# One FFN chunk normalized in transposed layout, a pair's inverse stage cut by columns, and a table turned by DMA

## The chip, the cores and the metric

The kernel runs on one core of a Trainium2 chip. The metric is the device time of one execution in microseconds. A core has five engines, each with its own queue of instructions: TensorE (PE, matrix products out of SBUF into PSUM; its weight loads are shown as PEld), VectorE (DVE), ScalarE (ACT), GpSimd (POOL), and SyncE (SP), which here issues all DMA transfers. An instruction waits at the head of its queue until the semaphores it needs are up; those behind it wait with it.

## What is computed

```python
x = A_x                                        # 1 x 2048 x 512, bf16
X = rfft2(layernorm(x)) * (A_w_r + 1j * A_w_i)
h = x + irfft2(X, (2048, 512)).astype(bf16)
u = layernorm(h)
r = relu(u @ B_w1 + B_b1)                      # 512 -> 1792
out = h + (r * r) @ B_w2 + B_b2                # 1792 -> 512
```

A layernorm takes off the mean over the 512 features and divides by sqrt(variance + 1e-5).

## The kernel before

Token 16 p + g lies on partition p, in group g (16 groups of 128 tokens). The two-dimensional transform is done as matrix products with tables of sines and cosines that the kernel makes itself.

- *Front.* x arrives in six transfers. For each group DVE (bn_stats) or ACT takes mean and variance; POOL raises the variance to the power -1/2; the first table KF is scaled by it (KR, L409). Stage 1 (s1, L416 and L417) multiplies each group by KR, and the result goes into Bt (L432, L448). The row means stay in nm1 with their sign turned; what the filter adds has a row mean of zero, so nm1 serves the second layernorm too.
- *Middle.* Eight pairs of frequency blocks, pr = 0 to 7. For each: stage 2 on PE with table GF (p2, L516), its eviction U on ACT (L526), stage 3 with table EF (p3, L495), its eviction AB on ACT (L593), then on DVE a butterfly X (L600, for the pairs that do it there), the product m with the filter weights W (L614), the complex combination Z in two halves (L624), and a fold M in two halves (L635, L637; pair 6 has none and takes Z itself). Stage 4 (p4) multiplies by the inverse table EI (L662; pair 6 in L659 also by EN, a negated slice), and T2 is its eviction (L677). p4 of pair 7 is made in two parts, each of half of the row table index; each part's eviction is cut into the columns of groups 0 and 1 (T2a) and of the others (T2b).
- *Drain, for the tokens of chunk 0 (groups 0 and 1).* Stage 5 with table GI (pd, L738) needs T2a of all pairs. Its evictions EO (L743) go into stage 6 with table KI (py, L828 to L833), which is accumulated on top of x. Group 0 gets its sum of squares on ACT (L689), group 1 its statistics by bn_stats on DVE (L843); then square root on ACT (L846), reciprocal, scaled offset, the normalized u (L857, L859), a transpose on PE through the identity (L868), and a copy to UT (L874). Then come the up products.
- *FFN.* Five chunks of groups, (0, 2), (2, 5), (5, 9), (9, 13), (13, 16). Up products ph/sg (L936), relu on ACT (L948), square on DVE (L954), down products po (L965), addition of hb on DVE (L974), output by SP. Stages 5 and 6 of the later groups (p5, L765 to L768; p6, L788 to L796) and their second layernorm are woven between.

The tables: EF and GF are sines by ACT from integer phases. EI0 and EI1 are EF turned by DMA (`tr_dma`, L453), EI2 is EI0 negated on ACT (L482), EN a negated slice on ACT (L485). GI is made directly: POOL makes its phases fiI (L469), ACT takes the sine (L260, at 35.5 in the profile).

*What sets the order.* All work is given to a planner, `Plan`, as tasks with an engine, an assumed duration, what it reads and writes, a priority and a pool slot. `plan.run` chooses at each step the task that can start first by its own assumed times, and emits it; the emitted order is then fixed for each engine (`pin`). In the middle the order is instead written out by hand for PE, ACT and DVE (`MID`). An assumed duration is not a time of the chip; it only decides the order. Transfers have assumed landing times (`lag`). When the planner sees a gap in front of a product it puts in products of zeros (`warm`, L243, and the loop in `bank`, L716), whose result is overwritten.

PSUM has eight banks: in the middle three double banks (mm) and two single ones (sg); in the FFN three pp, one ph, two po, two sg.

Of the kernel before, what the change touches and what calls it, by code (L numbers as in the profile page):

```python
# [9 lines left out]
ALU = mybir.AluOpType  # L10
# [23 lines left out]
class Plan:  # L34
# [55 lines left out]
    def run(self, line=None):  # L90
# [8 lines left out]
        while any(left.values()):  # L99
            best = None  # L100
            for e, ts in left.items():
                cand = []
                for t in ts if e not in lines else [t for t in ts if t["name"] == lines[e][0]] if lines[e] else []:
                    r = self.ready(t, e)
                    if r is None:
                        continue
                    if t["alloc"]:
                        s, _ = self.slot(t["alloc"][0])
                        if s is None:
                            continue  # L110
                        r = max(r, s)
                    r = max(r, self.free[e])
                    cand.append((r, t))
                    if r <= self.free[e] + 1e-9:
                        break
# [17 lines left out]
            if e in lines:  # L133
                lines[e].pop(0)
# [10 lines left out]
def kernel(  # L145
# [22 lines left out]
    BY_Z = (6,)  # L168
    L = D // 2
# [23 lines left out]
    mv2 = persist.tile([P, 2], FP32, name="mv2")  # L193
    st2 = persist.tile([P, 6], FP32, name="st2")
# [10 lines left out]
    EI = fwd.tile([P, 3, 9, P], BF16, name="EI")  # L205
    EN = fwd.tile([P, len(BY_Z), 2, P], BF16, name="EN")
# [20 lines left out]
    fiI = tab.tile([P, 4, 256], I32, name="fiI")  # L227
    idxD = tab.tile([P, 256], I32, name="idxD")
# [57 lines left out]
    for i in range(2):  # L286
        add("SP", 1.0, lambda i=i: sy.dma_start(W[:, 2 + i, 1:8], wx[i][:, ::-1]), reads=[("wx", i)], writes=[("Wr", i)],
            prio=10 + i, lag=10.5)
# [27 lines left out]
    pool(0.14, lambda: iota(pI[:, 5:7], [[128, 2]], 128, 256), 1.0, writes=["p2"])  # L316
# [4 lines left out]
    pool(0.34, lambda: iota(idxD[:], [[1, 256]], 0, 0), 395.0, writes=["idxD"], order=[("KR", G - 1)])  # L321
# [31 lines left out]
    for t in range(2):  # L353
        act(0.62, lambda t=t: sin_of(flat(GF[:, t]), lo(flat(fiG[:, t]))), 0.6 + t / 10, reads=[("fiG", t)],
            writes=[("gf", t)])
    dve(0.15, lambda: ve.tensor_scalar(GF[:, :, :, 255:256], GF[:, :, :, 255:256], 0.5, None, ALU.mult), 54.0, reads=[("gf", 0), ("gf", 1)],
        order=[("KR", G - 1)], writes=["GF"])
# [94 lines left out]
    def tr_dma(i, dst, src, dep, prio):  # L452
        add("SP", 2.5, lambda: sy.dma_start(dst, src, transpose=True), reads=dep, writes=[("EI", i)], prio=prio, lag=(10.6, 10.4, 0, 8.0)[i])  # L453
    for i in range(2):
        tr_dma(i, EI[:, i], flat(EF[:, i]), [f"EF{i}"], 12 + i)
    tr_dma(3, KI[:], flat(KF[:]), ["KF"], 16)
    for k, (d, s) in ((0, (W1[:], B_w1.rearrange("(c p) f -> p c f", p=P))),
# [3 lines left out]
            order=[("EI", i) for i in range(4)] + [("Wr", 0), ("Wr", 1), ("Wn", 0), ("Wn", 1)])  # L461
# [5 lines left out]
    dve(0.13, lambda: ve.tensor_copy(pF[:, 5:7], pI[:, 5:7]), 0.75, reads=["p2"], writes=["pF2"], shared=True)  # L467
    for lt in range(4):
        pool(0.48, lambda lt=lt: gp.tensor_scalar(fiI[:, lt], idxD[:], pF[:, 5 + lt % 2:6 + lt % 2],  # L469
                                                  float((QT, HT)[lt // 2]), ALU.mult, ALU.add), 400.0,  # L470
             reads=["pF2", "idxD", ("KR", G - 1)], writes=["fiI"])
# [5 lines left out]
    def mid_tasks():  # L477
        def b1t():
            mm(sg_tile(("b1",))[:, 0:NF], lhsT=b1b[:], rhs=ident[0:NF, 0:NF], start=True, stop=True)
        add("PE", 0.07, b1t, reads=["b1b", "ident"], order=[("p3", 3)], writes=[("b1",)], prio=141.0, alloc=("sg", ("b1",)))  # L480
        act(0.19, lambda: sc.copy(b1f[:], T[("b1",)][:, 0:NF]), 142.0, reads=[("b1",)], writes=["b1f"])
        act(1.1, lambda: sc.activation(flat(EI[:, 2]), flat(EI[:, 0]), ACT.Identity, scale=-1.0), 83.0, reads=[("EI", 0)],  # L482
            order=["EF2", ("X", 0, 0)], writes=[("EI", 2)])
        for pr in BY_Z:
            act(0.37, lambda pr=pr: sc.activation(EN[:, BY_Z.index(pr)], EI[:, 0:2, pr], ACT.Identity, scale=-1.0), 84.0,  # L485
                reads=[("EI", 0), ("EI", 1)], writes=[("EI", 3, pr)])
        act(1.07, lambda: sin_of(flat(GI[:]), lo(flat(fiI[:]))), 142.0, reads=["fiI"], order=[("p3", 4)], writes=["GI"])
        act(1.4, lambda: sc.activation(junk[:, 0:1], eps[:], ACT.Sqrt), 0.0, reads=["GI", "eps", ("p4", SQ)], writes=["sqrt"])
# [8 lines left out]
    for pr, first in ((0, 1), (1, 1), *((p, 0) for p in range(8))):  # L497
# [12 lines left out]
        if first or pr > 1:  # L510
# [7 lines left out]
            for q in range(2):  # L518
                add("PE", 0.46, lambda pr=pr, q=q, s2=s2: s2(pr, q), reads=["Bt", "GF"],
# [102 lines left out]
        def zz(pr=pr, r=0):  # L622
            Z = buf(fwd, ("Z", pr), "Z", [P, 2, 2, 256], BF16, 2) if r == 0 else T["Z", pr]
            ve.tensor_tensor(Z[:, :, r], T["m", pr][:, :, 0, r], T["m", pr][:, :, 1, 1 - r], (ALU.subtract, ALU.add)[r])  # L624
# [18 lines left out]
        def s4(pr, part, lts):  # L643
            key = ("p4", pr, "t", lts[0] // 2) if pr == 7 else ("p4", pr)
            pt = T[key] if part else (sg_tile if pr == 7 else mm_tile)(key)
            src = T["M" if pr and pr not in BY_Z else "Z", pr][:].rearrange("p u r (j e) -> p u r e j", e=2)
            for lt in lts:
                r, e = lt // 2, lt % 2
                k = lt - lts[0] if pr == 7 else lt
                o = pt[:, 256 * k:256 * k + 256]  # L650
                if pr == 0:
                    for u, k1 in ((0, 0), (1, 8)):
                        ou = o[:, P * u:P * u + P]
                        mm(ou, lhsT=src[:, u, r, e, :], rhs=EI[:, 1, k1, :], start=True, stop=False)
                        mm(ou, lhsT=src[:, u, 1 - r, e, :], rhs=EI[:, 2 if r == 0 else 0, k1, :], start=False, stop=True)
                elif pr in BY_Z:
                    for u in range(2):
                        i = 1 if r == part else 0 if u != r else 2
                        mm(o, lhsT=src[:, u, part, e, :], rhs=EI[:, i:i + 2, pr, :] if i < 2 else EN[:, BY_Z.index(pr)],  # L659
                           start=part == 0 and e == 0 and u == 0, stop=part == 1 and e == 1 and u == 1)  # L660
                else:
                    mm(o, lhsT=src[:, part, r, e, :], rhs=EI[:, 1 - part:3 - part, pr, :],  # L662
                       start=part == 0 and e == 0, stop=part == 1 and e == 1)
        for h in range(2):
            for k in range(2) if pr == 7 else (None,):
                lts = {None: range(4) if pr else (2 * h, 2 * h + 1), 0: (0, 1), 1: (2, 3)}[k]
                add("PE", 0.92 if pr in BY_Z else 0.46 if k is None else 0.23, lambda pr=pr, h=h, s4=s4, lts=lts: s4(pr, h, lts),
                    reads=[("Z", pr) if pr == 0 else ("ZM"[pr not in BY_Z] + "h" * (1 - h), pr), ("EI", 0), ("EI", 1), ("EI", 2)]
                    + [("EI", 3, pr)] * (pr in BY_Z), order=[("p4", pr, 0, k)] * h, uses=[("ZM"[pr > 0 and pr not in BY_Z], pr)],
                    writes=[("p4", pr, h, k)] + [("p4", pr)] * (k is None) + [("p4", pr, "t", k)] * (k is not None),  # L670
                    name=f"p4-{pr}-{h}" + "ab"[k] * 1 if k is not None else f"p4-{pr}-{h}", prio=z + 32 * (pr < 5),
                    alloc=(("mm", ("p4", pr)) if k is None else ("sg", ("p4", pr, "t", k))) if h == 0 else None)

        def et(eng=sc.copy, pr=pr, a=0, b=G, l0=0, l1=4):
            dst = T2[:, l0:l1, a:b, 2 * pr:2 * pr + 2, :].rearrange("p l g q s -> p l q g s")
            src = T["p4", 7, "t", l0 // 2] if pr == 7 else T["p4", pr]
            eng(dst, src[:].rearrange("p (l q g s) -> p l q g s", q=2, g=G, s=8)[:, :, :, a:b])  # L677
        if pr < 7:
# [331 lines left out]
```

## Time and profile before

| | |
|---|---|
| Time, median of 3 runs | 160.37 us (160.04 to 160.56) |
| The profiled execution | 160.21 us, of it 158.4 us span from first to last instruction |
| Granted TensorE clock | 1.000 |
| PE busy | 152.0 us (96%) |
| DVE busy | 119.0 us (75%) |
| ACT busy | 102.5 us (65%) |
| POOL busy | 33.1 us (21%) |
| Chain that ended last | PE 74%, DVE 15%, DMA 4%, issue 3% |

The busy shares over the span mix stages with different limits. The slices show it: each digit is a fortieth of the span, 4.0 us, in tenths busy, from left to right.

```profile
PE   6998999999798999999999999999999999999992
DVE  5999988999867987889952989991599962285221
ACT  8989679999967887297801899530588820188000
POOL 8798700000000033022240013440002240000000
DMA  4957999994000001104132000314000312010011
```

Until slice 5 the input arrives and the statistics are taken; slices 5 to 10 are the middle; slices 11 and 12 are the drain of chunk 0; from slice 13 on the FFN runs with a full PE. POOL is busy while tables are made and then empty until the FFN. The DMA engines are full up to slice 9, because the FFN's weights follow the filter's.

### The profile page before, as it was taken

The page shows a single profiled execution, that of the slowest core. Times are in us where ns is not written, and L with a number is a line of the kernel's source. Part 1 is how long each engine was busy: PE and PEld are TensorE (multiplying, and loading weights), DVE is VectorE, ACT ScalarE, POOL GpSimd, SP SyncE. Part 2 cuts the span into 40 slices and gives each one's busy share as a digit, 9 for nine tenths or more (in the row PEclk, how much of TensorE's full clock was granted, in tenths as well). Part 3 has the DMA queues.
Part 4 walks back from the last instruction along what each step waited for, and adds up shares of the span by engine and source line. Part 5 has one row for each costly group of instructions (what it writes and reads, how often), then busy time and mean ns, then how long its engine had stood idle before and what let it go on. Part 6 is the DMA issues. An engine that isn't in the chain of part 4 may idle for free.

```text
span 158.4 us, 2890 instructions
## 1 busy us (share of the span) xinstructions
PE 152.0 (96%) x1027; PEld 91.9 (58%) x1027; DVE 119.0 (75%) x322; ACT 102.5 (65%) x189; POOL 33.1 (21%) x83
## 2 busy tenths in 40 slices
PE   6998999999798999999999999999999999999992
PEld 4587876787477886565544544444544444565471
DVE  5999988999867987889952989991599962285221
ACT  8989679999967887297801899530588820188000
POOL 8798700000000033022240013440002240000000
DMA  4957999994000001104132000314000312010011
GB/s 128 320 187 219 242 226 218 387 363 140 0 4 0 0 4 35 35 33 35 35 66 67 33 0 4 66 35 132 33 0 0 69 36 66 33 35 4 0 66 33
DMA packets 21017, 13.43 MB, mean 85 GB/s; under 512 B 9738, under 2 KB 19722, under 8 KB 21002
## 3 DMA queue, kind: packets, MB, share of 16 engines
q1 hardware_dynamic: 21002, 13.25, 31.3%
q8 instruction: 8, 0.13, 0.3%
q14 instruction: 7, 0.06, 0.1%
HBM read 8.92 MB, written 3.01 MB: 75 GB/s over the span
## 4 chain that ended last, share of the span: by engine, by line
PE 74%; DVE 15%; DMA 4%; issue 3%; SPq 1%; ACT 1%; POOL 0%; ACTq 0%
PE po L965 31%; PE sg L936 20%; PE ph L936 10%; DMA xs<-in_A_x_dram 4%; DVE Z L624 3%; DVE m L614 3%; DVE st L393 3%; DVE X L600 2%; PE m_p L516 2%; PE pp L788 1%; DVE M L635 1%; PE pp L795 1%; SPq L272 1%; DVE M L637 1%; PE s_p L516 1%
## 5 line engine op out<-in xcount | busy, mean ns | idle before, releaser
L965 PE MATMUL po<-W,act 128*128 128x512 bf16 (+1 forms) x238 | 50.0, 366 | 0.0
L948 ACT ACTIVATE rl<-sg,b1f 128x384 bf16<-128x384 f32 (+2 forms) x46 | 27.3, 601 | 21.9 <-PE sg L936 20.6
L936 PEld LDWEIGHTS <-W 128*128 128x128 bf16 x288 | 26.8, 98 | 19.7 <-issue 0.2
L936 PE MATMUL sg<-UT,W 128*128 128x384 bf16 (+2 forms) x184 | 37.2, 337 | 0.0
L965 PEld LDWEIGHTS <-act 128*128 128x128 bf16 x238 | 23.2, 98 | 24.0
L954 DVE TENSOR_TENSOR act<-rl 128x384 bf16<-128x384 bf16 (+2 forms) x70 | 25.0, 367 | 6.5 <-ACT rl L948 6.0
L974 DVE TENSOR_TENSOR ot<-po,hb 128x512 bf16<-128x512 f32 (+1 forms) x17 | 11.2, 658 | 20.7 <-PE po L965 20.5
L880 POOL TENSOR_SCALAR rs<-ss 128x1 f32<-128x1 f32 x14 | 6.1, 435 | 90.5 <-ACT junk L689 90.5
L948 ACT ACTIVATE rl<-ph,b1f 128x512 bf16<-128x512 f32 (+2 forms) x23 | 13.8, 602 | 10.0 <-PE ph L936 9.4
L936 PE MATMUL ph<-UT,W 128*128 128x512 bf16 (+3 forms) x96 | 19.9, 330 | 0.1
L816 DVE TENSOR_TENSOR hs<-pp,xs 128x512 bf16<-128x512 f32 x14 | 9.6, 689 | 2.3 <-PE pp L788 1.3
L689 ACT ACTIVATE junk<-hs,nm 128x512 bf16<-128x512 bf16 x14 | 10.0, 714 | 0.1
L495 PE MATMUL m_p<-U,EF 128*128 128x512 bf16 (+1 forms) x46 | 9.5, 337 | 0.0
L393 DVE BATCH_NORM_STATS2 st<-xs 128x6 f32<-128x512 bf16 x14 | 9.0, 672 | 0.6 <-DMA xs<-in_A_x_dram 0.6
L811 DVE TENSOR_TENSOR R<-q 128x127 bf16<-128x127 f32 x40 | 9.4, 283 | 0.0
L820 DVE TENSOR_TENSOR hb<-hs,b2b 128x512 f32<-128x512 bf16 x14 | 9.1, 681 | 0.0
L882 POOL TENSOR_TENSOR rs<-rs,mhalf 128x1 f32<-128x1 f32 x14 | 8.0, 569 | 1.2
L778 DVE TENSOR_TENSOR q<-pp,od 128x256 f32<-128x256 f32 x20 | 7.6, 415 | 0.0
L243 PEld LDWEIGHTS <-fz 128*128 128x128 bf16 x59 | 5.0, 113 | 4.2 <-issue 2.3
L516 PE MATMUL m_p<-GF,Bt 128*128 128x256 bf16 x56 | 7.4, 273 | 0.0
L677 ACT CAST T<-m_p 128x1024 bf16<-128x1024 f32 x7 | 7.1, 1057 | 0.5 <-PE m_p L659 0.5
L593 ACT CAST AB<-m_p 128x1024 bf16<-128x1024 f32 x7 | 7.3, 1046 | 0.0
(163 smaller groups left out, 227.6 us busy)
## 6 DMA issues: line engine op xcount, KB each, us to landing
W<-in_B_w_dram SPq DMA_DIRECT2D x2, 1792.0 KB, 10.7
out_dram<-ot SPq DMA_DIRECT2D x15, 128.0 KB, 1.8
xs<-in_A_x_dram SPq DMA_DIRECT2D x4, 256.0 KB, 3.8
xs<-in_A_x_dram SPq DMA_DIRECT2D x2, 512.0 KB, 6.7
W<-wx SPq DMA_DIRECT2D x2, 448.0 KB
W<-in_A_w_r_dram SPq DMA_DIRECT2D x1, 512.0 KB, 8.0
W<-in_A_w_i_dram SPq DMA_DIRECT2D x1, 512.0 KB, 6.4
wx<-in_A_w_r_dram SPq DMA_DIRECT2D x1, 448.0 KB
```

Source lines behind the costliest of these rows:

```text
L393: ve.bn_stats(st[:], xs[:, g, :])
L495: mm(o.rearrange("p (j i e) -> p j i e", e=2, i=RUN), lhsT=w, rhs=U[:, q, s].rearrange("p (j e i) -> p j i e", e=2, i=RUN), **k)
L516: mm(puv[:, e, :], lhsT=Bt[:, 2 * t + 1 - e, 2 * pr + q, :], rhs=gfv[:, t, :, e, :], start=(t == 0), stop=(t == 1))
L689: sc.activation(junk[:], src, ACT.Square, bias=nm1[:, g:g + 1], accum_out=ss2[:, g:g + 1])
L811: ve.tensor_tensor(o, x, y, (ALU.add, ALU.subtract, ALU.subtract, ALU.add)[k])
L816: dve(0.66, lambda g=g: ve.tensor_tensor(hs[:, g, :], T["p6", g][:], xs[:, g, :], ALU.add), z, reads=[("p6", g)], writes=[("hs", g)])
L820: add(("DVE", "POOL")[HBP], (0.62, 1.3)[HBP], lambda g=g: (ve, gp)[HBP].tensor_tensor(hb[:, g, :], hs[:, g, :], b2b[:], ALU.add), prio=lat ...
L936: mm(p[:, P * i0:P * i1], lhsT=W1[:, d, bass.ts(f, P)], rhs=T["UT", c][:, i0:i1, d, :], start=(d == 0), stop=(d == ND - 1))
L948: sc.activation(r[:, 0:P * n], T["ph", c, f][:, 0:P * n], ACT.Relu, bias=b1f[:, f:f + 1], scale=1.0)
L954: ve.tensor_tensor(t[:, f, 0:P * n], r[:, 0:P * n], r[:, 0:P * n], ALU.mult)
L965: mm(p[:, cs], lhsT=T["act", c][:, f, bass.ts(i, P)], rhs=W2[:, f, cs], start=(f == 0), stop=(f == NF - 1))
L974: ve.tensor_tensor(o[:, cs], T["po", g, h][:, cs], hb[:, g, cs], ALU.add)
```

## The change

It has several parts, made together.

- **Chunk 0 is made transposed.** A bank yt per group holds features on partitions and tokens on columns. PE accumulates into it: the means taken off (a product of two rows of ones with nmt, the sign-turned means split into two bf16 parts), x through the identity, and stage 6 with EO as the stationary side. ACT squares the bank, PE sums over partitions with a matrix of ones, so that every partition has each token's sum, ACT takes 1/std as Exp(-0.5 Ln(sum/512 + eps)), and DVE multiplies into UT0, which is the FFN's operand. The py products for the residual stay, and come after it. The transposes on PE, the copies, bn_stats, the root and the reciprocals of chunk 0 go.
- **Stage 4 of pair 7 is cut by columns**: part a has the columns of groups 0 and 1 for all four row indices (32 wide), part b the rest (2 x 112 wide).
- **Stage 5 of chunk 0** makes one tile per group of both halves, evicted in one copy each.
- **GI is GF turned by DMA** (two transposes), then two of its four blocks are multiplied on POOL by hrow (1, in the last row 0.5). The phases fiI on POOL, the sine on ACT and the halving of GF on DVE (L356) go.
- **EI2 is EF2 turned by DMA**, and the negated slice for pair 6 is a turned block of CN, in place of two ACT instructions. The reversed filter weights (W from wx) are issued before these transposes.
- **Z of pair 6** is stored with the two halves one behind the other, not interleaved.
- **Table set**: one load of the set that has logarithm and exponential takes the place of the load for the square root.
- **Orders**: MID is written anew, and the first instructions after it are also written out (DRAIN), after which the planner goes on by itself. The PSUM pools pp/ph and po are allocated in the other order.

```diff
     def tr_dma(i, dst, src, dep, prio):
-        add("SP", 2.5, lambda: sy.dma_start(dst, src, transpose=True), reads=dep, writes=[("EI", i)], prio=prio, lag=(10.6, 10.4, 0, 8.0)[i])
+        add("SP", 2.5, lambda: sy.dma_start(dst, src, transpose=True), reads=dep, order=[("EI", 2)] * (i == 3) + [("Wr", 1)] * (i < 2), writes=[("EI", i)], prio=prio, lag=(10.6, 10.4, 6.0, 6.0)[i])
...
+    tr_dma(2, EI[:, 2], flat(EF[:, 2]), ["EF2"], 15)
+    for pr in BY_Z:
+        add("SP", 1.2, lambda pr=pr: sy.dma_start(EI[:, 3, pr], CN[:, pr - PE0], transpose=True), reads=["CN"],
+            order=[("EI", 3)], writes=[("EI", 3, pr)], prio=17, lag=6.0)
+    for t in range(2):
+        add("SP", 1.3, lambda t=t: sy.dma_start(GI[:, :, P * t:P * t + P], flat(GF[:, t]), transpose=True), reads=[("gf", t)],
+            order=[("EI", 3)], writes=[("gi", t)], prio=40.5 + t / 10, lag=12.0)
...
-        act(1.1, lambda: sc.activation(flat(EI[:, 2]), flat(EI[:, 0]), ACT.Identity, scale=-1.0), 83.0, reads=[("EI", 0)],
-            order=["EF2", ("X", 0, 0)], writes=[("EI", 2)])
-        act(1.07, lambda: sin_of(flat(GI[:]), lo(flat(fiI[:]))), 142.0, reads=["fiI"], order=[("p3", 4)], writes=["GI"])
-        act(1.4, lambda: sc.activation(junk[:, 0:1], eps[:], ACT.Sqrt), 0.0, reads=["GI", "eps", ("p4", SQ)], writes=["sqrt"])
+        act(1.4, lambda: sc.preload_act_table_set("natural_log_exp_and_others"), 0.0, reads=["eps"], writes=["sqrt"])
+        for e in range(2):
+            pool(0.5, lambda e=e: gp.tensor_scalar(GI[:, 1 + 2 * e], GI[:, 1 + 2 * e], hrow[:], 1.0, ALU.mult, ALU.mult), 410.0,
+                 reads=["hv", ("gi", 0), ("gi", 1)], writes=["GI"], name=f"GI-{e}")
...
-            ve.tensor_tensor(Z[:, :, r], T["m", pr][:, :, 0, r], T["m", pr][:, :, 1, 1 - r], (ALU.subtract, ALU.add)[r])
+            ve.tensor_tensor(Z[:, r] if pr in BY_Z else Z[:, :, r], T["m", pr][:, :, 0, r], T["m", pr][:, :, 1, 1 - r],
+                             (ALU.subtract, ALU.add)[r])
...
+    def cen(g):
+        mm(sg_tile(("yt", g))[:], lhsT=ones[0:2, :], rhs=nmt[:, g].unsqueeze(1).to_broadcast([2, ND, P]), start=True, stop=False)
+    def res(g):
+        for d in range(ND):
+            mm(T["yt", g][:, P * d:P * d + P], lhsT=xs[:, g, P * d:P * d + P], rhs=ident[:], start=False, stop=False)
...
+        def yt6(g=g, k=0):
+            o = T["yt", g][:].rearrange("p (a d c) -> p d a c", a=2, c=P)
+            for d in range(2):
+                mm(o[:, d], lhsT=EO[:, g, k, P * d:P * d + P],
+                   rhs=KI[:] if k else KI[:, 0].unsqueeze(1).to_broadcast([P, 2, P]), start=False, stop=k == 1 and d == 1)
...
+        act(0.6, lambda g=g: sc.activation(flat(sq0[:, g]), T["yt", g][:], ACT.Square), -30.0, reads=[("yt", g, 3)],
+            writes=[("sq", g)], uses=[("yt", g)])
+        def ssm(g=g):
+            p = mm_tile(("ss", g))
+            for d in range(ND):
+                mm(p[:, 0:P], lhsT=ones[:], rhs=sq0[:, g, d], start=d == 0, stop=d == ND - 1)
...
+        act(0.3, lambda g=g: sc.activation(rsb[:, g], T["ss", g][:, 0:P], ACT.Ln, bias=eps[:], scale=1.0 / D), -30.0,
+            reads=[("ss", g), "sqrt"], writes=[("sd", 0, g)])
+        act(0.26, lambda g=g: sc.activation(rsb[:, g], rsb[:, g], ACT.Exp, scale=-0.5), -30.0, reads=[("sd", 0, g)],
+            writes=[("r2", 0, g)])
+        def ut0(g=g):
+            ve.tensor_tensor(UT0[:, g], T["yt", g][:].rearrange("p (d c) -> p d c", c=P),
+                             rsb[:, g].unsqueeze(1).to_broadcast([P, ND, P]), ALU.mult)
...
     MID = {
-        "PE": "p2-2-0 p2-2-1 p3-1 p2-3-0 p2-3-1 p3-2 p2-5-0 p2-5-1 p3-3 p2-6-0 b1 p2-4-0 p2-4-1 p3-5 "
-             "p2-6-1 p3-4 p4-0-0 p4-0-1 p4-1-0 p4-1-1 p2-7-0 p2-7-1 p4-2-0 p4-2-1 p3-6 p3-7 p4-3-0 "
-             "p4-3-1 p4-5-0 p4-5-1 p4-4-0 p4-4-1 p4-6-0 p4-6-1 p4-7-0a p4-7-0b p4-7-1a p4-7-1b",
-        "ACT": "U-2 AB-1 U-3 AB-2 U-5 AB-3 EI-2 b1f U-4 AB-5 U-6 AB-4 T2-0 T2-1 U-7 GI EI-3-6 AB-6 T2-2 "
-              "AB-7 T2-3 T2-5 sqrt T2-4 T2-6 T2a-0 T2b-0",
+        "PE": "p3-1 p2-2-0 p2-2-1 p2-4-0 p2-4-1 p2-3-0 p3-2 p2-3-1 p3-4 p2-6-0 p2-6-1 p3-3 p4-0-0 b1 "
+             "p4-0-1 p3-6 p2-5-0 p2-5-1 p2-7-0 p2-7-1 p4-2-0 p4-2-1 p4-1-0 p4-1-1 p3-5 p3-7 p4-3-0 "
+             "p4-3-1 p4-4-0 p4-4-1 p4-6-0 yt-0-0 p4-6-1 p4-5-0 yt-0-1 p4-5-1 p4-7-0a p4-7-1a p4-7-0b "
+             "pd-0 pd-1 yt-1-0 yt-1-1 yt-0-2 yt-0-3 yt-1-2 yt-1-3 p4-7-1b ss-0 ss-1",
+        "ACT": "AB-1 U-2 U-4 AB-2 U-3 AB-4 U-6 b1f AB-3 nmt T2-0 AB-6 U-5 U-7 T2-2 sqrt AB-5 T2-1 AB-7 "
+              "T2-3 T2-4 T2-6 T2-5 T2a-7 EO-0 EO-1 sq-0 sq-1 sd-0-0 r2-0-0 sd-0-1 r2-0-1 T2b-7-1",
...
     }
...
-    plan.run()
+    DRAIN = {
+        "PE": "py-1-0 py-0-0 py-1-1 py-0-1 py-1-2 py-0-2 pf-0 pf-1 p5-2 ph-0-0 ph-0-1 p5-3 ph-0-5 "
+             "ph-0-3 ph-0-2",
+        "ACT": "od-2 rl-0-0 rl-0-1 od-3 rl-0-5",
+        "DVE": "hb-1 hb-0 q-2-0 q-2-1",
+    }
+    plan.run(DRAIN)
```

## The prediction

> **What bounds the kernel now.** I read the table of windows first, then the waits, then the chain of waits.
>
> In the windows (stretch, mean, then busy us of PE, weight loads, DVE, ACT, POOL, the clock, the DMA share and GB/s) the middle part has three full engines and an empty POOL:
>
> ```profile
> 24.00:28.00 4.00, 4.00 (x30) 2.64 (x28) 3.50 (x8) 4.00 (x6) 0.00 (x0) 1.00 1.00 218
> 36.00:40.00 4.00, 4.00 (x33) 2.94 (x30) 4.00 (x8) 4.00 (x6) 0.00 (x0) 1.00 0.35 110
> 48.00:52.00 4.00, 3.45 (x53) 2.90 (x52) 3.47 (x11) 3.05 (x8) 0.00 (x0) 1.00 0.00 0
> ```
>
> The chain says which of the three counts. From 24.46 to 44.68 it is DVE with short PE pieces. Then comes a serial drain, here cut to its ends (start, us, what):
>
> ```profile
> 44.40 1.05 PE s_p L662 x8
> 45.45 0.56 PE pp L716 x10
> ...
> 50.67 0.43 DVE UT L874
> ...
> 51.15 0.38 PE ph L936 x4
> ...
> 52.31 0.96 PE sg L936 x8
> ```
>
> From 52.31 on PE is never idle: 103.11 us up to 155.42, then the last output. So nothing counts but (a) when DVE ends its last fold (M of pair 7, 44.68; I call this moment t0) and (b) how long after t0 PE is full. PE's idle shows only as filler: L716, 10 and 17 empty matmuls.
>
> DVE in the middle has two waits that an order can remove (engine line, what it waited for, us in total, times, longest):
>
> ```profile
> DVE X L600 <- ACT AB L593: 0.6, 1, 0.6
> ...
> DVE Z L624 <- PE m_p L659: 0.4, 1, 0.4
> ```
>
> **The front (−0.2).** The scaling of GF leaves DVE. The chain has it at 16.70 with 0.20, between the last KR and the first Bt copy, and PE's s_p at 17.53 hangs on that copy; the copy starts at 16.61 instead of 16.80, as its own matmuls were done by 16.4. The pF cast (0.16 at 4.88) stands before the wait for x that the chain has until 8.96, so it gives nothing.
>
> **The middle, DVE (−0.8).** The new order puts p3-1 ahead of p2-2 on PE and AB-1 ahead of U-2 on ACT. p3-1 starts one p2 (0.87) earlier, so AB-1 ends by about 23.6, when DVE ends Z-0 (23.85): the 0.61 before X goes. Z of pair 6 is stored half by half, so the second half no longer overlaps what p4-6-0 reads: the 0.44 at 42.79 goes. Counts of X, m, Z and M stay. Against that, the new DVE order has two or three more neighbours of which the second reads the first: such a pair starts 0.44 apart (43.92 after Z), independent ones 0.34; I charge 0.25. Together −0.8: t0 = 44.68 − 0.2 − 0.8 = 43.7.
>
> **ACT and POOL.** ACT loses the negated EI (1.22), EN (0.46) and the sine of GI (1.11), gains nmt (about 0.4), and one table load (1.28) replaces the other. That is 2.4 us off a full engine, but DVE ends the stage, so I count it at nothing beyond the above; it is what lets the evictions come on time. fiI and idxD leave POOL (1.84 and 0.35). POOL gains small operations before 21 us, and two products on GI (128x256 bf16, hrow), which cannot run before GI lands.
>
> **SP and the queue.** In the built order SP issues: both W from wx, EI0, EI1, EI2 (new), KI, one CN block (new), W1, two GI (new), W2, b2b. The rows for issues are these:
>
> ```profile
> 16.10 3.30 SPq L453 DMA_TRANSPOSE EI<-EF  x1
> 19.50 1.22 SPq L287 DMA_DIRECT2D W<-wx  x2
> 20.77 2.59 SPq L453 DMA_TRANSPOSE EI<-EF  x1
> 23.46 1.19 SPq L453 DMA_TRANSPOSE KI<-KF  x1
> ```
>
> The first four issues change places only, so EI2 is issued at 23.46, until 26.05. Who waits for it is p4-0-0, which the new PE list has early: after p3-3, which waits for U-3. ACT's evictions start 0.91 apart (25.22, 26.12, 27.02): AB-1 22.4, U-2, U-4, AB-2 (0.2 late, on p3-2), U-3 ends 27.3; p3-3 adds 0.87. Need: 28.3. If EI2 is late, p3-6 and all later PE work stand behind p4-0-0 and DVE runs dry: every us is a us. Lower bound of the landing: 26.05 + 1.2 (a UT turn: 2.4 to landing, 1.2 of it issue) = 27.3. Upper: 23.46 + 5.9, the landing of both EI = 29.4. The second EI had both W transfers ahead of it in a full queue (DMA share 1.0); EI2 has only turns ahead, so I take 27.8: no wait. Here a rule speaks against the change: the Trainium skill, "VectorE: DVE Perf Modes", § The three transpose paths, has 1309 ns for a 128x128 turn by DMA against 390 ns on TensorE. Nine blocks would be 11.8 us (an estimate from that page), EI2 would land at 35.2, and the kernel would be 6 us slower. The row has nine blocks in 5.9 us, traffic included; the row decides.
>
> Behind EI2 and CN, W1 goes from 24.69 to about 28 and lands near 36 (7.8 us after issue: the two FFN weights have a median of 10.7, the later one 13.6); it is needed at 49. GI lands behind it, about 37; needed at t0 + 0.8. W2 and b2b move some 5 us, from at most 39.3 (25.87 + 13.4) to 44.5; b2b is needed at 50. All are covered; if a cover were gone, the delay would count in full.
>
> **The two products on POOL (+0.5).** They fall at 37 to 38, into DVE's full stretch. The trace shows POOL and DVE excluding each other. DVE's EF negation beside POOL's fiI took 697 ns and ended 0.32 after fiI's end at 19.11. Conversely a one-element POOL instruction, 223 ns by its median, took 1.94 beside DVE instructions with two SBUF inputs:
>
> ```profile
> 101.09 1.94 POOL L880 TENSOR_SCALAR rs<-ss 128x1 f32<-128x1 f32 x1 [2.60 <-ACT junk L689]
> ```
>
> It ended when the second hb of L820 did (102.98). The rule is the Trainium skill, "SBUF — State Buffer", § SBUF: two separate sides: a VectorE instruction with two SBUF inputs and a GpSimd one that reads SBUF take turns, whoever starts first holds the ports for its whole instruction. By the rule DVE pays two whole products, 2 x 0.48 (POOL's KR row, same shape) = 0.96. By the 101.09 row DVE pays nothing, since POOL is held off, and the products run after t0, ready at t0 + 1.0. But POOL was let in between neighbours too (the L880 at 126.86 ended at 127.54, inside a run of hb), so it will be within the dozen changes of instruction that follow 37. I take 0.5, about half an instruction each; ends 0 and 0.96.
>
> **The drain (−0.2).** From t0, by rows: four 32-column matmuls 0.49 (128 columns: 219 ns; narrower ones are not in the trace, so this is the upper bound, the lower 0.05 less); T2a, 128 columns on ACT, 0.27 (64 are 218 ns, 256 are 372) and 0.04 of hop: 0.80. pd-0: 0.69 (load 0.1, three steps of 0.108, 272 ns): 1.49; pd-1 1.92. EO, both on ACT (585 ns, 0.49 apart): 2.12, 2.60. yt-1: 3.29. Squares (585 to 687; I take 0.6): 3.45, 3.94. Column sums by the ones matrix: 3.95, 4.42. Ln-0 0.31, Exp-0 0.28 (between 295 ns of the root and 372): 4.60. UT0-0, 679 ns like hb L862: 5.31. Ready for the first up at 5.4. But PE is full from 4.25: the six py groups of the residual, 1.30 (four of 0.217, four of 0.108), end at 5.55. So the first up is at t0 + 5.55; the same sum for the old drain gives about 0.2 less than its 6.47, so I take 5.8. UT0-1 (5.95) hides behind two ups and a p5. After it PE has 103.11 + 0.87 (sixteen 128-column ups) + 0.68 (three p5 groups, which before ran in the gap at 48.0) = 104.66. PE's end: t0 + 110.46, against 44.68 + 110.74 now: −0.28, rounded to −0.2. Two norm chains became one chain of whole-bank steps, transposes and UT copies are gone, but PE work that was filler time is now paid: hence so little.
>
> **Sum.** −0.2 − 0.8 + 0.5 − 0.2 = −0.7. The profiled execution is 160.21 (span 158.4 and 1.8 around it): 159.5. The median of the runs is 160.37, 0.16 above it: I say **159.6**. A difference under 0.3% (0.48 us) can't be told from none.
>
> **Rivals.**
> - *The ports cost nothing* (POOL starves or slips into gaps): −1.2, 159.1. For: the 101.09 row. Against: the 126.86 one. Chance 0.20.
> - *The ports cost the whole 0.96* and the drain gives nothing: 160.2, no change. For: EF's row, which waited for the very end of a POOL instruction. Chance 0.13.
> - *EI2 comes late: slower.* Place: p4-0-0. Price: one us for each past 28.3; from 29.0 on the gain is gone. For: 5.9 from issue gives 29.4, and SP has stood 4.75 us in one wx issue and 5.20 in b2b against 0.5 to 1 in like ones. One such stall of 2 us: EI2 at 29.8 to 30.3, 160.4 to 161.5; I say 161.1. Against: the transfer eight places ahead, for which its issue waits, has landed by 17.8 (9.82 + 8.0). Chance 0.22.
> - *Ln and Exp reload tables*, two loads of 1.28 in the drain: excluded, the built order has two loads in all, as before.
>
> **How the numbers follow.** Forecast 0.45, own range 159.2 to 160.0. Faster by over 0.3%: 0.39 of it and the 0.20 = 0.59. Slower: 0.20 of the late EI2. Same: 0.06 + 0.13 + 0.02 = 0.21. Range for 8 in 10: 158.9 (ports free, drain 0.2 better) to 161.0 (EI2 2 us late).
>
> **What would show it.** Right: no DVE wait at X L600 nor at pair 6's Z; last fold at 43.9 to 44.5; two POOL products near 37 with a DVE instruction 0.3 to 0.5 longer beside each; first up 5.6 to 6.0 after the last fold; no PE idle after it. Wrong: PE waiting at p4-0-0 for a DMA, or POOL's products so late that pd waits for GI.

## The result and the profile after

| | before | after |
|---|---|---|
| Time, median | 160.37 us (160.04 to 160.56) | 159.28 us (158.99 to 159.67) |
| Ratio | | 0.9938, 95% interval 0.9916 to 0.9960 |
| The profiled execution | 160.21 us, span 158.4 | 158.99 us, span 157.2 |
| First m of the middle starts | 21.77 | 21.23 |
| First m to the end of the last fold | 22.91 | 22.30 |
| Last fold's end to the first up | 6.47 | 5.95 |
| First up to the end of the last PE group | 104.23 | 104.72 |
| PE busy, DVE busy | 152.0, 119.0 us | 152.0, 116.4 us |

The change makes the kernel 1.09 us faster by the medians, 0.64 to 1.35 by the interval. Forecast were 159.6 and a range of 158.9 to 161.0. The profiled execution of after is the fastest of its five runs, and the lower four rows show why its own difference (1.2) is not all due to the change: 0.54 of it lies ahead of the first m, where, as shown below, executions of the same front code differ by up to 0.9 us.

The windows of after, same columns as before (stretch, length, then busy us of PE, weight loads, DVE, ACT, POOL, the clock, the DMA share and GB/s):

```profile
24.00:28.00 4.00, 4.00 (x28) 2.38 (x26) 3.90 (x8) 3.80 (x5) 0.00 (x0) 1.00 0.72 144
36.00:40.00 4.00, 4.00 (x34) 3.11 (x33) 4.00 (x10) 3.72 (x5) 3.04 (x1) 1.00 1.11 336
48.00:52.00 4.00, 4.00 (x46) 3.21 (x44) 3.63 (x10) 3.02 (x10) 0.00 (x0) 1.00 0.00 0
```

DVE went from 3.50 to 3.90 in the first stretch: the wait at X is gone. ACT, full before, has room. POOL is busy in the second stretch for 3.04 us with a single instruction. The third stretch, in which PE had 3.45, is full.

The chain of waits of after through the drain (start, us, what; cut to its stations):

```profile
43.19 0.35 DVE M L649
...
43.59 0.27 PE s_p L675 x4
...
44.63 0.87 PE m_pd L707 x8
...
46.15 0.87 PE s_yt L730 x8
...
47.83 0.32 PE m_ss L743 x4
48.15 0.56 PE po L880 x2
...
49.47 0.11 PE po L885
49.58 0.28 PE ph L952 x4
```

By the profile it runs on PE from the fold to the first up. What ends last ahead of the up is the residual (po, L880 to L885), not the product UT0, which DVE makes from 48.44 to about 49.13. Part b of pair 7's stage 4 (47.03) and filler (44.24, not shown) stand in this chain too, while ACT makes T2a, EO and the squares. The filler is a little in the way: T2a is there at 44.26, and pd's first product starts at 44.47.

### The profile page after: what moved, and what is told of

The parts are those of the page before. It is cut to its first block, busy times and chain, and to the rows that moved or that the text cites. A ratio compares the mean times of both kernels' runs of the same rounds, so it can differ in the third digit from the quotient of the medians.

```text
span 157.2 us, 2915 instructions
## 1 busy us (share of the span) xinstructions
PE 152.0 (97%) x1038; PEld 92.5 (59%) x1038; DVE 116.4 (74%) x310; ACT 102.0 (65%) x187; POOL 37.7 (24%) x84
## 3 DMA queue, kind: packets, MB, share of 16 engines
HBM read 8.92 MB, written 3.01 MB: 76 GB/s over the span
## 4 chain that ended last, share of the span: by engine, by line
PE 75%; DVE 14%; issue 3%; POOL 3%; DMA 2%; ACT 0%; DVEq 0%
PE po L981 31%; PE sg L952 20%; PE ph L952 11%; DVE Z L635 4%; DVE m L625 4%; DMA xs<-in_A_x_dram 2%; DVE X L611 2%; DVE st L395 2%; POOL KR L411 1%; PE pp L840 1%; DVE M L649 1%; DVE M L647 1%; POOL rs L402 1%; PE pp L847 1%; PE s_p L418 1%
## 5 line engine op out<-in xcount | busy, mean ns | idle before, releaser
L964 ACT ACTIVATE rl<-sg,b1f 128x512 bf16<-128x512 f32 (+2 forms) x46 | 27.4, 602 | 20.1 <-PE sg L952 19.1
L952 PE MATMUL sg<-UT,W 128*128 128x512 bf16 (+3 forms) x188 | 37.6, 334 | 0.0
L952 PE MATMUL ph<-UT,W 128*128 128x384 bf16 (+3 forms) x100 | 20.5, 328 | 0.0
L964 ACT ACTIVATE rl<-ph,b1f 128x384 bf16<-128x384 f32 (+2 forms) x24 | 14.3, 596 | 8.2 <-PE ph L952 7.5
L495 POOL TENSOR_SCALAR GI<-GI,hrow 128x256 bf16<-128x256 bf16 x2 | 6.0, 2986 | 17.5 <-DMA GI<-GF 17.5
L689 ACT CAST T<-m_p 128x1024 bf16<-128x1024 f32 (+1 forms) x8 | 7.5, 955 | 0.8 <-PE m_p L673 0.7
L908 ACT ACTIVATE u<-hs,nr,rs 128x512 bf16<-128x512 bf16 x5 | 4.1, 811 | 5.9 <-POOL nr L900 5.9
L246 PEld LDWEIGHTS <-fz 128*128 128x128 bf16 x69 | 5.5, 108 | 3.8 <-issue 1.6
```

Of the source, the lines that this page charges most:

```text
L952: mm(p[:, P * i0:P * i1], lhsT=W1[:, d, bass.ts(f, P)], rhs=T["UT", c][:, i0:i1, d, :], start=(d == 0), stop=(d == ND - 1))
L964: sc.activation(r[:, 0:P * n], T["ph", c, f][:, 0:P * n], ACT.Relu, bias=b1f[:, f:f + 1], scale=1.0)
```

## The experiments

In the table below the stretches are read from the profiled execution; the ratio is that of the times to the kernel before. "Folds" is the first m to the end of the last fold, "up" from there to the first up. The edits are cut to the lines that matter; "..." stands for what is left out, such as the adjusted dependencies.

| kernel | ratio, 95% interval | first m | folds | up |
|---|---|---|---|---|
| before | 1 | 21.77 | 22.91 | 6.47 |
| after | 0.9938 (0.9916 to 0.9960) | 21.23 | 22.30 | 5.95 |
| a_noprod | 0.9947 (0.9932 to 0.9963) | 21.86 | 22.13 | 5.97 |
| a_giact | 0.9943 (0.9922 to 0.9964) | 22.14 | 22.14 | 5.96 |
| a_zinter | 0.9958 (0.9943 to 0.9972) | 22.02 | 22.29 | 5.96 |
| a_front | 0.9942 (0.9920 to 0.9964) | 21.54 | 22.29 | 5.95 |
| a_wlate | 0.9976 (0.9958 to 0.9993) | 21.78 | 22.90 | 5.94 |
| a_nosplit | 1.0044 (1.0022 to 1.0067) | 21.61 | 22.28 | 7.43 |
| a_ei2w1 | 1.0561 (1.0525 to 1.0598) | 21.52 | 32.77 | 6.26 |
| a_best | 0.9931 (0.9917 to 0.9946) | 21.68 | 22.13 | 5.81 |
| b_order | 1.0020 (1.0003 to 1.0037) | 22.03 | 23.25 | 6.47 |
| b_zhalf | 0.9971 (0.9951 to 0.9991) | 21.49 | 22.87 | 6.47 |
| b_both | 0.9975 (0.9961 to 0.9990) | 21.79 | 22.78 | 6.48 |
| b_mid | 0.9981 (0.9968 to 0.9995) | 22.05 | 22.80 | 6.47 |

The folds column repeats to 0.02 where nothing in that stage was changed (after, a_front, a_nosplit: 22.28 to 22.30; a_noprod, a_giact and a_best: 22.13 to 22.14), though by the intervals the times of two kernels can be told apart only from about 0.3 us on. So verdicts on tenths rest on this column and on the waits, and the ratios only have to agree.

### The two POOL products: a_noprod and a_giact

```diff
-            pool(0.5, lambda e=e: gp.tensor_scalar(GI[:, 1 + 2 * e], GI[:, 1 + 2 * e], hrow[:], 1.0, ALU.mult, ALU.mult), 410.0,
...
```

> The changed kernel without the two POOL products on GI (the halving of the table's last row is left out). From the first m to the end of the last fold the changed kernel takes 22.30 us. Theory (POOL was held off by VectorE for 6 us and cost VectorE only the Z and M instructions beside which it got in, 0.2 to 0.25): 22.05 to 22.15, the kernel 0.2 us faster than the changed one. Rule (whole products, 0.96): 21.35, some 0.9 us faster. The prediction's half way (0.5): 21.8. Ports free: 22.30, no change.

```diff
-            pool(0.5, lambda e=e: gp.tensor_scalar(GI[:, 1 + 2 * e], GI[:, 1 + 2 * e], hrow[:], 1.0, ALU.mult, ALU.mult), 410.0,
+        act(0.6, lambda: sc.activation(GI[:, 1::2], GI[:, 1::2], ACT.Identity, scale=hrow[:]), 410.0,
...
```

> The changed kernel with the halving of GI's last row as one ScalarE instruction (128x512, about 0.6 us) in ScalarE's 0.73 us of idle time ahead of T2 of pair 6, none on POOL. Theory: VectorE gets back its 0.2 to 0.25 (first m to last fold 22.1), ScalarE's T2 of pair 6 is not later, 0.2 us faster than the changed kernel (near 159.0). Rival (the idle time was shorter than the instruction and its hop; T2-6 and with it T2a come later): no change or 0.2 slower.

In the timeline of after, POOL and then DVE (start, us, engine, line, operation, what it writes and reads, shapes, count, idle time before):

```profile
36.96 5.96 POOL L495 TENSOR_SCALAR GI<-GI,hrow 128x256 bf16<-128x256 bf16 x2 [17.52 <-DMA GI<-GF]
```

```profile
41.29 0.41 DVE L649 TENSOR_TENSOR M<-Z 128x512 bf16<-128x512 bf16 x1
41.74 0.92 DVE L635 TENSOR_TENSOR Z<-m 128x512 bf16<-128x512 bf16 x2
42.76 0.43 DVE L647 TENSOR_TENSOR M<-Z 128x512 bf16<-128x512 bf16 x1
```

and the same Z in a_noprod:

```profile
42.37 0.76 DVE L632 TENSOR_TENSOR Z<-m 128x512 bf16<-128x512 bf16 x2
```

The first product took 5.09 us and the second 0.88. That it is DVE that holds them up shows in a_ei2w1 (below), where DVE happens to be idle when GI lands:

```profile
37.44 0.94 POOL L495 TENSOR_SCALAR GI<-GI,hrow 128x256 bf16<-128x256 bf16 x2 [17.72 <-DMA GI<-GF]
```

Both take 0.94 there, 0.48 the first, as KR's row has it. In after the first one ends 20.82 us after the first m, beside the Z at 41.74; that Z starts 0.03 after the end of the M ahead of it, DVE's first pause since POOL had its data. In a_zinter, a_front and a_nosplit the first product started 15.3 to 15.7 us after the first m and ended 20.81 to 20.82 after it, and in a_wlate 0.6 later, as DVE itself is there: what lets it in is a place in DVE's order. In after DVE paid 0.16, all at one Z (0.92 for 0.76): folds 22.30 with the products, 22.13 without. Of the four expectations the first holds. a_giact's theory holds too. On ACT the product is free: it takes 0.74, runs in the idle time from 42.04 on, and T2 of pair 6 starts 20.76 after the first m, to the hundredth as in after. The ratios of these kernels, 0.9943 and 0.9947, do not show the 0.17; it is below what they resolve.

### The orders and the waits of the middle: b_order, b_zhalf, b_both, a_zinter

```diff
-        "PE": "p2-2-0 p2-2-1 p3-1 p2-3-0 ...
+        "PE": "p3-1 p2-2-0 p2-2-1 p2-3-0 ...
-        "ACT": "U-2 AB-1 U-3 ...
+        "ACT": "AB-1 U-2 U-3 ...
```

> The kernel before with two moves in the written orders alone: p3-1 ahead of p2-2 on TensorE, AB-1 ahead of U-2 on ScalarE. Theory: the 0.61 wait of VectorE at the first X after AB goes, first m to last fold 22.91 to 22.3, 0.5 to 0.6 us faster than before. Rival (U-2 and so p3-2 come one eviction later, and the wait turns up again at the X of pair 2): under 0.2 us.

The theory failed. The wait at the first X is gone, and a longer one stands at the next, as the timeline of DVE in b_order shows:

```profile
24.03 0.75 DVE L600 TENSOR_TENSOR X<-AB 128x512 bf16<-128x512 bf16 x2
24.82 1.23 DVE L614 TENSOR_TENSOR m<-X,W 128x2048 bf16<-128x2048 bf16 x1
26.80 0.42 DVE L600 TENSOR_TENSOR X<-AB 128x512 bf16<-128x512 bf16 x1 [0.75 <-ACT AB L593]
```

U-2 was put one eviction later, so p3-2 and AB-2 are later (AB-2 starts 3.72 after the first m, for 3.45 in before), and DVE, which reaches the first X 0.69 earlier after the first m, asks for AB-2 sooner. The folds take 23.25, 0.34 longer than before. In after AB-2 is as late (3.73), but DVE makes both Z and the first M of pair 1 ahead of that X and never asks early.

```diff
-            ve.tensor_tensor(Z[:, :, r], T["m", pr][:, :, 0, r], T["m", pr][:, :, 1, 1 - r], (ALU.subtract, ALU.add)[r])
+            ve.tensor_tensor(Z[:, r] if pr in BY_Z else Z[:, :, r], T["m", pr][:, :, 0, r], T["m", pr][:, :, 1, 1 - r], (ALU.subtract, ALU.add)[r])
...
```

> The kernel before with pair 6's Z stored half by half; nothing else. Theory: the 0.44 wait of VectorE at the second half of Z of pair 6 goes and the last fold ends 0.4 earlier: 0.4 us faster than before. Rival (the second half then starts at once but p4-6 and what follows on TensorE has not moved, and the drain waits for TensorE instead): under 0.15 us.

The wait at pair 6's Z went, and in the profiled execution another came, in the DVE timeline of b_zhalf:

```profile
24.18 0.76 DVE L600 TENSOR_TENSOR X<-AB 128x512 bf16<-128x512 bf16 x2 [0.60 <-ACT AB L593]
25.39 1.23 DVE L614 TENSOR_TENSOR m<-X,W 128x2048 bf16<-128x2048 bf16 x1 [0.44 <-DMA W<-wx]
```

The filter weights from wx land at about 25.4 here. This execution was 0.28 ahead of the one of before at the first m, so it ran into them; in the profile of before m started at 25.25 and saw nothing of it. So the landing of W stands right behind the wait at X. By the times b_zhalf is 0.46 faster (0.14 to 0.79), as the theory has it; the folds of the profile (22.87) are those of an execution with the W wait.

```diff
-        "PE": "p2-2-0 p2-2-1 p3-1 p2-3-0 ...
+        "PE": "p3-1 p2-2-0 p2-2-1 p2-3-0 ...
...
-            ve.tensor_tensor(Z[:, :, r], ...
+            ve.tensor_tensor(Z[:, r] if pr in BY_Z else Z[:, :, r], ...
```

> The kernel before with both: the two moves in the orders, and pair 6's Z half by half. Theory (the two waits add up): first m to last fold 22.91 to 21.9, about 1.0 us faster than before, that is as fast as the whole change or 0.1 faster than it, since the rest of the change gave 0.1 and cost 0.2 at the ports. Rival (the waits shift rather than go): 0.5 us or less.

Folds 22.78, 0.40 us faster by the ratio: the rival's number. A wait at m for W and one at the second X stand in place of the 0.61, in b_both's DVE timeline:

```profile
24.93 1.22 DVE L614 TENSOR_TENSOR m<-X,W 128x2048 bf16<-128x2048 bf16 x1 [0.39 <-DMA W<-wx]
26.55 0.43 DVE L600 TENSOR_TENSOR X<-AB 128x512 bf16<-128x512 bf16 x1 [0.40 <-ACT AB L593]
```

a_zinter takes the storage of Z back in the changed kernel:

```diff
-            ve.tensor_tensor(Z[:, r] if pr in BY_Z else Z[:, :, r], T["m", pr][:, :, 0, r], T["m", pr][:, :, 1, 1 - r],
+            ve.tensor_tensor(Z[:, :, r], T["m", pr][:, :, 0, r], T["m", pr][:, :, 1, 1 - r],
...
```

> The changed kernel with pair 6's Z stored interleaved again, as before; nothing else. Theory (the 0.44 wait of before was worth its full length): a VectorE wait of 0.3 to 0.5 at the second half of pair 6's Z comes back, the last fold 0.3 to 0.5 later, 0.4 us slower than the changed kernel. Rival (in the new order p4-6-0 reads the first half early or late enough that nothing waits): no change.

The rival holds: no DVE wait at Z, folds 22.29. In the new order the storage does nothing; the order alone removes this wait, and in the old order the storage alone does.

### What else the waits needed: a_wlate and b_mid

```diff
- ... order=[("EI", 2)] * (i == 3) + [("Wr", 1)] * (i < 2), writes=[("EI", i)] ...
+ ... order=[("EI", 2)] * (i == 3) + [("EI", 1)] * 0, writes=[("EI", i)] ...
...
- ... writes=[("Wr", i)],
+ ... order=[("EI", 0)], writes=[("Wr", i)],
```

> The changed kernel with SyncE's order put back at one place: the first turn of EF into EI ahead of the two W transfers from wx, as before; nothing else. Theory (the wait at the first X could go only because the change also issues these transfers earlier; in the kernels built from before they landed at 24.9 to 25.4, 6 us after issue, and m of pair 1 is due 2.80 us after the first m, at 24.0 to 24.9): VectorE waits 0.3 to 1.0 for W at m of pair 1, first m to last fold 22.6 to 23.3, the kernel 0.3 to 1.0 us slower than the changed one. Rival (as the prediction had it, these issues change places only): no wait for W, 22.3, no change.

The theory holds. The queue of SyncE in after:

```profile
16.67 1.54 SPq L290 DMA_DIRECT2D W<-wx  x2
18.27 6.45 SPq L455 DMA_TRANSPOSE EI<-EF  x3
```

The same in a_wlate, and what its DVE then meets:

```profile
15.95 3.04 SPq L455 DMA_TRANSPOSE EI<-EF  x1
19.09 1.22 SPq L290 DMA_DIRECT2D W<-wx  x2
```

```profile
25.18 1.23 DVE L625 TENSOR_TENSOR m<-X,W 128x2048 bf16<-128x2048 bf16 x1 [0.64 <-DMA W<-wx]
```

The two transfers are issued 2.4 us later and DVE waits 0.64 for them; folds 22.90, the whole gain of the middle lost, and the ratio goes from 0.9938 to 0.9976, 0.6 us.

```diff
-        "DVE": "... m-1 X-2-0 Z-1-0 Z-1-1 X-2-1 M-1-0 M-1-1 X-3-0 ...
+        "DVE": "... m-1 Z-1-0 Z-1-1 M-1-0 X-2-0 X-2-1 M-1-1 X-3-0 ...
...
+ ... order=[("Wr", 1)] * (i < 2), ...
```

(with the edits of b_both)

> The kernel before with four edits in the middle stage alone: p3-1 and AB-1 early; on VectorE both Z and the first M of pair 1 ahead of the X of pair 2; the two W transfers issued ahead of both EI turns; pair 6's Z half by half. The last stage, the norm and the tables stay as before. Theory (the two waits go only with all of these): no wait of VectorE at X, m or Z, first m to last fold 21.9 to 22.2 (22.91 less 0.61 less 0.44, and some dependent neighbours), the drain 6.47 as before, 0.7 to 1.0 us faster than before, as fast as the whole change. Rival (a new wait at the X of pair 3, whose eviction is later): 22.4 or more, 0.5 us or less.

The rival holds. The DVE timeline of b_mid:

```profile
28.67 0.43 DVE L600 TENSOR_TENSOR X<-AB 128x512 bf16<-128x512 bf16 x1 [0.33 <-ACT AB L593]
...
32.97 0.76 DVE L624 TENSOR_TENSOR Z<-m 128x512 bf16<-128x512 bf16 x2 [0.27 <-PE m_p L655]
```

Both waits can be read against after. The first waits for the third AB eviction, which starts 5.57 after the first m here (27.62, of pair 3) and 5.54 in after (26.77, of pair 4): it is no earlier there, but DVE makes m of pair 2 ahead of that X. Up to it ACT has done the same number of evictions in both kernels, so what ACT was relieved of has no part in this wait. The second waits for a Z buffer that p4 of pair 0 still reads. That p4 starts 9.83 after the first m here, 6.63 in after. From ACT and PE in b_mid:

```profile
28.52 1.18 ACT L482 ACTIVATE EI<-EI 128x1152 bf16<-128x1152 bf16 x1
31.88 0.22 PE L654 MATMUL m_p<-EI,Z 128*128 128x128 bf16 x1
```

At 6.63 it could not stand here, since ACT makes EI2 until 29.70, 7.65 after the first m. But what keeps it until 9.83 is its place in PE's order, 2.2 us after EI2 is there and with PE busy all the time. So neither wait shows that EI2 had to come by DMA. What these runs tell is this: the two moves, W early, pair 6's storage and DVE's new start do not make the gain of the middle by themselves; the rest of the new lists is needed. How it divides between the order of the pairs and the evictions that ACT was relieved of was not tried.

### The front: a_front

```diff
+    dve(0.15, lambda: ve.tensor_scalar(GF[:, :, :, 255:256], GF[:, :, :, 255:256], 1.0, None, ALU.mult), 54.0, reads=[("gf", 0), ("gf", 1)],
+        order=[("KR", G - 1)], writes=["GF"])
...
```

> The changed kernel with one VectorE instruction on GF's last columns (by 1.0, so the values stay) back at its old place between the last KR and the first Bt copy. The first m started at 21.23 in the changed kernel, at 21.77 before. Theory (the instruction costs its 0.2, the other 0.34 of the front was the arrival of x in that one execution): from the last KR's start to the first m 0.2 longer, 0.2 us slower. Rival (the whole 0.54 of the front hangs on the instruction): 0.5 us slower. Rival (hidden): no change.

From the KR group behind POOL's last rs to the first stage 2 product it is 2.73 us here, and 2.73 to 2.74 in four of the five other kernels with the instruction; without it 2.65 to 2.66 in six of eight. (Apart stand after with 2.78, a_giact with 2.99 and b_order with 2.98.) So it is worth 0.08, nearer to "hidden" than to the 0.2 expected: the four Bt copies of DVE that follow take 2.14 in place of 2.01, since they now wait for PE between them. The rest of the front's 0.54 is the arrival of x: DVE's statistics waited 0.6 for it in before, 1.0 in a_zinter and 0.05 in after. One row of before, a_zinter and after each:

```profile
8.96 1.29 DVE L393 BATCH_NORM_STATS2 st<-xs 128x6 f32<-128x512 bf16 x2 [0.19 <-DMA xs<-in_A_x_dram]
```

```profile
9.33 1.29 DVE L395 BATCH_NORM_STATS2 st<-xs 128x6 f32<-128x512 bf16 x2 [0.73 <-DMA xs<-in_A_x_dram]
```

```profile
8.36 1.29 DVE L395 BATCH_NORM_STATS2 st<-xs 128x6 f32<-128x512 bf16 x2
```

Over all eight kernels without the instruction the first m starts at 21.23 to 22.14, on average 21.73; over six with it at 21.49 to 22.05, on average 21.78.

### The late EI2: a_ei2w1

```diff
- ... order=[("EI", 2)] * (i == 3) + [("Wr", 1)] * (i < 2), ...
+ ... order=[("EI", 1)] * (i == 3) + [("FW", 0)] * (i == 2) + [("Wr", 1)] * (i < 2), ...
...
```

> The changed kernel with the third EI turn issued behind W1. Theory (the rival of the late EI2 was a true price: whatever comes later than p4-0-0 needs it is paid in full, and a turn behind W1 lands behind W1's data): EI2 issued at 27 to 28 and landed near 35 to 36, as GI did at 36.3; p4-0-0 waits from 27.9 to then, the kernel 6 to 8 us slower than the changed one. Rival (a turn overtakes the bulk of W1, landing 2.3 to 3.3 us after issue as the EI turns did, at 30): 1.5 to 2.5 us slower. Rival (TensorE has slack to catch up): under 1 us.

Slower by more than the highest of these: 10 us (1.0561 against 0.9938). Its SyncE queue, its waits (engine line, what it waited for, us in total, times, longest) and two of its windows:

```profile
26.78 0.57 SPq L469 DMA_DIRECT2D W<-in_B_w_dram  x1
27.40 3.92 SPq L455 DMA_TRANSPOSE EI<-EF  x1
```

```profile
PE m_p L669 <- DMA EI<-EF: 7.2, 1, 7.2
DVE Z L635 <- PE m_p L669: 6.9, 1, 6.9
...
DVE M L647 <- PE m_p L675: 3.3, 1, 3.3
```

```profile
28.00:36.00 8.00, 1.20 (x18) 0.93 (x16) 3.75 (x7) 1.01 (x2) 0.00 (x0) 0.76 1.08 280
36.00:44.00 8.00, 7.64 (x48) 5.30 (x48) 2.90 (x6) 4.00 (x6) 0.94 (x2) 0.60 0.84 267
```

The clock in windows of 1 us:

```profile
31.00:32.00 1.00, 0.00 (x0) 0.00 (x0) 0.75 (x2) 0.00 (x0) 0.00 (x0) 1.00 1.03 403
32.00:33.00 1.00, 0.00 (x0) 0.00 (x0) 0.00 (x0) 0.00 (x0) 0.00 (x0) 0.57 0.98 376
41.00:42.00 1.00, 1.00 (x4) 0.45 (x3) 0.59 (x1) 0.00 (x0) 0.00 (x0) 0.50 1.10 375
43.00:44.00 1.00, 1.00 (x12) 0.90 (x10) 0.00 (x0) 0.91 (x2) 0.00 (x0) 1.00 0.06 20
```

The turn landed 8.9 us after its issue, at 36.3, 1.0 after W1 itself (35.3); with W1 behind it, in after, the same turn lands 3.28 us after issue. The second product of p4-0-0 came 8.5 us later than in after (36.36 for 27.91), and DVE lost 6.9 and then 3.3 more. Beside the second loss stands the clock: PE stopped at 29.2, the granted clock was 1.00 until 32, fell in the next microsecond and was 0.50 until 42, that is for almost 6 us after products started again. A 128x128 product takes 311 ns there for 219. The mean clock of all six executions is lower too, 0.968 to 0.980 for 1.000 in those of after. At full clock the 7.64 us at 0.60 would be 4.6, an estimate, so up to 3 us are the slow restart. The stall is paid in full, and the restart stands on top of it; how much of the 3 us DVE would have lost anyway was not tried.

### The drain: a_nosplit and a_best

```diff
-    SP4 = (7,)
+    SP4 = ()
...
- ... p4-7-0a p4-7-1a p4-7-0b pd-0 pd-1 yt-1-0 yt-1-1 yt-0-2 yt-0-3 yt-1-2 yt-1-3 p4-7-1b ss-0 ss-1
+ ... p4-7-0 p4-7-1 pd-0 pd-1 yt-1-0 yt-1-1 yt-0-2 yt-0-3 yt-1-2 yt-1-3 ss-0 ss-1
...
```

> The changed kernel with pair 7's stage 4 undivided: eight products of 256 columns, then one 128x1024 copy into T2 on ScalarE, then pd. By rows: second half of the products 0.55 in place of 0.49, the copy 1.0 in place of 0.27, so pd starts 0.8 later. Theory: first up 0.8 us later after the last fold (6.7 for 5.95), some of the products that the split puts into the gap no longer run there, but as many are not left for later, so the whole is 0.6 to 0.8 us slower than the changed kernel. Rival (the drain is bound by TensorE work and not by the chain): 0.2 or less.

The first up is 1.48 later, and the ratio is 0.0106 higher, 1.7 us. The chain to UT0 is 0.94 longer (49.74 less 43.89, for 48.44 less 43.53), near the 0.8 expected. The other half is a wait that nobody expected, in its PE timeline:

```profile
50.02 0.38 PE L880 MATMUL po<-xs,ident 128*128 128x512 bf16 x1 [0.57 <-ACT rsb L745]
```

The residual's first product waits for ACT's second logarithm, which reads the second sum of squares. That fits one bank for both. In after the product starts at 48.12, ahead of that logarithm's end (48.67), so its bank there is another; why the allocation falls so was not followed. The split is worth 1.5 us here, a third of it, by this reading, through the place of a bank. It is so against an undivided stage; the kernel before already had pair 7 in two parts, cut another way. What the transposed norm is worth by itself no run shows.

a_best goes on from a_giact: p4-7-1b ahead of pd, both T2 copies of part b on DVE, and the sums of squares in a pp bank so that py can start between them.

```diff
- ... p4-7-0b pd-0 pd-1 yt-1-0 yt-1-1 yt-0-2 yt-0-3 yt-1-2 yt-1-3 p4-7-1b ss-0 ss-1
+ ... p4-7-0b p4-7-1b pd-0 pd-1 yt-1-0 yt-1-1 yt-0-2 yt-0-3 yt-1-2 yt-1-3
...
-        "PE": "py-1-0 py-0-0 py-1-1 ...
+        "PE": "py-1-0 ss-0 py-0-0 ss-1 py-1-1 ...
...
```

> The changed kernel with GI's last row halved on ScalarE; the last part of pair 7's stage 4 (p4-7-1b) put into the filler time ahead of pd; its two T2 copies both on VectorE, which idles there; and the sums of squares in a bank of the next stage, so that the first two products of py run between them in place of filler. Theory: first m to last fold 22.14; the first up 5.6 to 5.7 after the last fold (bound by the chain through UT0, 5.6) for 5.95; together 0.4 to 0.5 us faster than the changed kernel. Rival (the new banks wait for those of the stage before, or the later orders that the planner makes anew lose time): the drain as long as now or longer, no gain.

The first up comes 5.81 after the last fold, 0.14 earlier, and now it is UT0 that it waits for:

```profile
49.62 0.38 PE L953 MATMUL ph<-UT,W 128*128 128x128 bf16 x4 [0.16 <-DVE UT L795]
```

Part b and three filler products left ahead of pd put pd, and with it the whole chain, 0.16 later after the fold (1.10 for 0.94). Together with the ports that is 0.3 by the stretches (folds 22.13, up 5.81); by the times, 159.13 for 159.28, it can't be told from after.

## Why the prediction was right

Term by term, with the stretches of the runs beside the steps:

| term | predicted | measured |
|---|---|---|
| front | −0.2 | −0.08 |
| DVE waits of the middle | −1.05 | −1.06 |
| dependent neighbours | +0.25 | +0.28 |
| ports | +0.5 | +0.17 |
| drain | −0.2 | −0.03 |
| sum | −0.7 | −0.7 |

(The neighbours are a_noprod's folds, 22.13, less those of before without its waits, 22.91 − 0.61 − 0.45. The drain is −0.52 at the first up and +0.49 behind it.) The sum of the stretches is that of the prediction; the median fell by 1.09, and its interval reaches down to 0.64. Three terms were off, by +0.12, −0.33 and +0.17, and cancelled: that the sum agrees to a tenth is luck. (160.37 less 0.7 is 159.67, where the prediction says 159.6.) Of its signs, the last fold came at 43.53, ahead of the 43.9 to 44.5 named, since x was early in this execution.

- *Front.* The step took DVE's start of the Bt copies for the path. The start moved by 0.2, but PE and ACT ended the stage. The term is 0.08.
- *Middle.* The two waits went, and the neighbours cost what was charged: in a_noprod's trace six instructions of DVE in this stretch start behind the end of the one ahead with no other wait (0.03 to 0.10 us), in before three. But the step that named the cause was wrong twice. It let the X wait go through two moves on PE and ACT; b_order made just these, and the wait came back at the next X, 0.14 longer. And it said of SP's issues that they "change places only" and gave the earlier W no worth: a_wlate shows that without this change of places 0.6 of the gain is lost. What came next behind the removed wait, W's landing and AB-2, was not asked for when the wait was counted. Pair 6's storage was not needed either (a_zinter).
- *ACT relieved.* Costed at nothing beyond letting evictions come on time. No run shows more: b_mid, with EI2 still on ACT, loses 0.33 through DVE's order and 0.27 through the place of p4-0 in PE's order. Whether the evictions could keep up in the new lists with EI2 on ACT was not tried.
- *EI2.* Right: its turn was issued at 23.44 and landed at 26.71, over 1 us ahead of p4-0-0 (27.86) and ahead even of the lower bound of 27.3. That is 3.28 us for nine blocks, so the rows were a better guide than the 11.8 estimated. The price was too low: 10 us for 8.5; what fits the difference is the clock after PE's idle time.
- *Ports.* The sum took half of each product where the row at 101.09 said none. The row was the nearer one: POOL was held off for 5 us and let in where DVE paused, at the tenth change of instruction ("within the dozen" was right), and took 0.16. The rule that whoever starts first has the ports for a whole instruction (the Trainium skill, "SBUF — State Buffer", § SBUF: two separate sides), read so that the one who waits is next, would have let the first product in at DVE's next change of instruction; nine passed ahead of the one that did. GI was ready at 42.92, ahead of the last fold, and pd did not wait for it.
- *Drain.* The first up was predicted at 5.8 after the fold, and is at 5.95; PE's work behind it was 104.66 predicted, 104.72 measured. The step that slipped is yt-1: predicted to end at 3.29, it ended at 3.50 (47.03), since EO of group 0 was ready at 45.69, but PE made the means and x of group 1 until 46.15 and only then all eight products of EO, 0.87 where the sum has 0.69. Squares, sums, UT0 and residual inherit it: sums at 4.62 for 4.42. The residual starts behind the sums, where the sum had it from 4.25 on, and ends at 6.05 for 5.55 and the 0.25 allowed.

## What to carry to other kernels

A wait that a reordering removes is worth its length only up to the next thing that was hidden behind it: before counting it, list for the consumer's next three instructions when each of their inputs comes, transfers included. A new product on POOL beside a VectorE that never pauses cost VectorE little here (0.17), but took ten times its length, so it must not be needed soon. The start of an execution varies with the arrival of its input; compare kernels by stretches between fixed instructions, not by spans.

## What the runs showed that was not expected

- A 128x256 POOL product took 5.09 us beside back-to-back DVE instructions with two SBUF inputs, 0.48 elsewhere. In five profiles the two products together took 5.96 to 6.67, and 0.94 in the one where DVE was idle.
- The DMA turn for EI2, nine blocks, landed 3.23 to 3.31 us after issue in the seven kernels with only turns right ahead of it, 3.98 in a_wlate, and 8.92 with the 1792 KB of W1 ahead. The first turn of EF, with the filter weights right ahead of it, took 5.3 to 5.9 in the five kernels that issue it so.
- With 7.2 us without products the granted clock fell to 0.50 about 3 us after the last one, and came back to 1.00 only about 6 us after products had started again.
- The first m of the same front code started anywhere from 21.23 to 22.14 in eight profiled executions. DVE's waits for x, 0.05 to 1.02 us, go most of the way with it.
